# Fourth lead tile turned by a transposing transfer between B's two, lead filled with the third column tile and two input products of 384 tokens

## The chip, the cores and the metric

One core of a Trainium2 chip runs the whole kernel. The metric is the device time of one execution in microseconds (us). TensorE is called PE here, VectorE DVE, ScalarE ACT, GpSimd POOL; SP is the engine whose queue issues nearly all transfers.

## The reference

The input is x, 2048 tokens of 512 features in bf16. Three things are added up: x itself, a diagonal state-space layer (S5) on the normalised x, and a gated feed-forward network on the same normalised x.

```python
xn = (x - mean(x)) / sqrt(var(x) + 1e-5)              # per token, 2048 x 512
dt = exp(log_dt); Lam_bar = exp(dt * (Lambda_re + 1j * Lambda_im))
Bu = einsum("bld,pd->blp", xn, ((Lam_bar - 1) / Lam)[:, None] * (B_re + 1j * B_im))
h_t = Lam_bar * h_{t-1} + Bu_t                        # 2048 steps, 512 states
y = 2 * einsum("blp,dp->bld", h, C_re + 1j * C_im).real + xn * Dskip
ffn = (gelu(xn @ w_gate) * (xn @ w_up)) @ w_down      # inner width 1376
out = x + y + ffn
```

## The kernel before

The tokens are cut into 16 tiles of 128 and four blocks of four tiles. For every block the kernel makes the normalised tiles XN (tokens on partitions), turns them into XNT (features on partitions), and then runs three families of matmuls: GU (gate and up products, 11 column tiles of the inner width, line 787), Bu (the input products of the state-space layer, four row tiles of B's real part and four of its imaginary part, line 730) and DN (the down product with the state-space output added to it in the same bank, lines 860 and 871). ACT takes gate and up out of PSUM (Gelu and copy, lines 795 and 797), DVE multiplies them (line 799), rotates and scans the states (CHAIN, lines 758 to 779) and adds up the output (line 878).

The order of the work comes from a small planner in the kernel. Every operation is recorded with its engine, an assumed duration, and the buffers that it reads and writes; from the buffers the planner derives what waits for what. PE and SP keep the order in which the program records; DVE, ACT and POOL are put in order by due times, except where `S.pin` fixes the order by hand. Buffers can be declared in parts, so that a reader waits for the part alone: `XNTt[t]` is one turned tile, `XNTh[t][h]` half of one, `bank_part` a stretch of columns of a PSUM bank.

The first block is handled apart, since at the start everything has to be loaded. This is the lead:

- SP issues, in this order: the four x tiles of the first block (one transfer each), two parameter rows, gate and up chunk 1, `ld_tr(BBT[0], "A_B_re")` and `ld_tr(BBT[1], "A_B_im")` (transfers from memory that turn their 512x512 matrix on the way, line 483), gate and up chunk 2, the x tiles of the second block (`ld_x(4, 4)`), chunks 3 and 4, and the x tiles of the third block. Gate and up chunk 0 and a parameter row go by ACT's queue. A queue issues in order: an issue that waits holds up all that are behind it.
- `LN_lead` normalises the four tiles on DVE (lines 538, 539, 554, 567), with the square root on ACT or POOL.
- `TR_lead(tt)` turns a tile on PE: four transposes of 128x128 into PSUM (line 598), which ACT copies to XNT (line 607). All four lead tiles are turned so. Tiles 0 and 1 use two banks each, tile 2 bank 6, tile 3 bank 7.
- `lead_half` (line 620) makes GU products of column tiles 0 and 1 for one token tile, from one half of the features; `lead_mm(pairs, t0, t1, which)` makes GU products of the named column tiles for token tiles t0 to t1 (gate, up or both). Column tile k uses banks 2k and 2k + 1.
- `TR_par` turns the parameter rows into the second half of bank 7 (line 630); ACT reads them out there (lines 668 to 674).
- `BU(0)` then makes the eight input products, each of four matmuls of 512 columns (line 730), in the banks 6, 7, 0, 1, 2, 3, 4, 5: `bu_mm` the product, `bu_out` its eviction, the first two on ACT and six on DVE. The four products with B_re come first.

After the lead, `LN(1, False)` takes the statistics of the second block's tiles on DVE and normalises them, and `TR(1)` turns each of them by one transposing transfer from on-chip memory to on-chip memory on SP's queue (line 655); blocks 2 and 3 are turned in the same way.

Of the kernel before, what the change touches and what calls it, by code (L numbers as in the profile page):

```python
# [308 lines left out]
NT, NB, KD, KP, KF = 16, 4, 4, 4, 11  # L309
# [18 lines left out]
def d_act(n, ptr=0): return 100.0 + 0.833 * n + 90.0 * ptr  # L328


def build(nc, ins, out):
    with ExitStack() as es:
        E = es.enter_context
        S = Sched(nc, es)
# [26 lines left out]
        XNT = [Buf("XNT%d" % b, "xnt", 4 * b, 4 * b + 4, XNT_all.ap[:, b]) for b in range(NB)]  # L361
# [102 lines left out]
        def ld_x(t0, n, queue="sync"):  # L464
            return load(X_all.ap[:, t0:t0 + n, :], x2[128 * t0:128 * (t0 + n), :].rearrange("(j p) d -> p j d", p=128),
                        n * 128 * 1024, X[t0:t0 + n], "ld_x", queue)
# [15 lines left out]
        def ld_tr(dst, nm):  # L482
            return S.dma(lambda e: e.dma_start_transpose(dst.ap, ins[nm]), 4.0 * 1000 * 330, writes=[dst], tag="tr_" + nm,
                         issue=1900.0, lat=1000.0)

        def ld_gu(ci):
            ld_w(WG, WGc, ins["B_w_gate"], ci)
            ld_w(WU, WUc, ins["B_w_up"], ci)
# [7 lines left out]
        ld_param(2, "A_Lambda_im")  # L496
        ld_gu(1)
        ld_tr(BBT[0], "A_B_re")
        ld_tr(BBT[1], "A_B_im")
        ld_gu(2)  # L500
        ld_x(4, 4)
        ld_gu(3)
        ld_gu(4)
        ld_x(8, 4)

        def late_loads():
            load(WD.ap[:, 0:10, :], ins["B_w_down"][0:1280, :].rearrange("(k p) d -> p k d", p=128),
# [68 lines left out]
        def LN_lead():  # L576
            st = [stats(tt) for tt in range(4)]
            rs = {0: rsqrt_act(0)}
            ln = [[center_half(0), center_half(1)]]
            for tt in range(1, 4):  # L580
                if tt == 2:
                    rsqrt(RQt[0][tt], MVt[0][tt].ap[:, 1:2], [MVt[0][tt]], 1)
                else:
                    rs[tt] = rsqrt_act(tt)
                ln.append([center(tt)])
            S.pin(*st[0], *st[1], *ln[0], *ln[1], *st[2], *st[3], *ln[2], *ln[3])
            return rs

        def TR_lead(tt, after=()):
            banks = ((6, 7), (4, 5), (6,), (7,))[tt]  # L590
            nd, ne = KD // len(banks), (2, 2, 2, 4)[tt]
            parts = [bank_part(bank, 0, 256 * nd) for bank in banks]
            for h, bank in enumerate(banks):
                def f(e, h=h, bank=bank):
                    ins_ = None
                    for i in range(nd):
                        dk = nd * h + i
                        ins_ = e.transpose(PSH[bank][:, 128 * i:128 * i + 128], XN[tt].ap[:, 128 * dk:128 * dk + 128], IDN.ap)  # L598
                    return ins_
                S.op("tensor", f, 100 * nd, [XN0h[h] if tt == 0 else XN[tt], IDN], [parts[h]], "T0", after)  # L600
                if tt == 0:
                    warm_pe(1, (128, 384)[h], 3)
            ev = []
            for g in range(KD // ne):
                h, c0 = divmod(ne * g, nd)
                pt = PSH[banks[h]][:, 128 * c0:128 * (c0 + ne)]
                ev.append(ACT(lambda e, g=g, pt=pt: e.activation(  # L607
                    XNT[0].ap[:, ne * g:ne * g + ne, 128 * tt:128 * tt + 128], pt.rearrange("p (k t) -> p k t", k=ne), ACTF.Copy),
                    d_act(128 * ne), [parts[h]], [XNTt[tt] if ne == KD else XNTh[tt][g]], "evT"))
            return ev  # L610

        def lead_half(t, h, which=(0, 1)):
            c0, c1 = 128 * t, 128 * t + 128

            def f(e):
                ins_ = None
                for dk in range(2 * h, 2 * h + 2):
                    for k in range(2):
                        for i in which:
                            ins_ = e.matmul(PS[2 * k + i][:, c0:c1], (WG, WU)[i].ap[:, dk, 128 * k:128 * k + 128],  # L620
                                            XNT[0].ap[:, dk, c0:c1], start=(dk == 0), stop=(dk == KD - 1))
                return ins_
            PE(f, d_pe([128] * 4 * len(which)), [(WGc, WUc)[i][0] for i in which] + [XNTh[t][h]],
               [bank_part(2 * k + i, 4 * c0, 4 * c1) for k in range(2) for i in which], "GU0")
# [24 lines left out]
                    cs.append(center(tt))  # L649
            return cs  # L650

        def TR(b):
            for j in range(4):
                tt = 4 * b + j
                S.dma(lambda e, b=b, j=j, tt=tt: e.dma_start_transpose(
                    XNT[b].ap[:, :, 128 * j:128 * (j + 1)], XN[tt].ap),
                    300 * 1024, reads=[XN[tt]], writes=[XNTt[tt]], tag="tr_x", issue=1270.0, lat=1400.0)

        (TH, RRr, LBR, LBI, N1, TAa, TBb, DEN, RDEN, TC, TD, NRE, TE, TF, NIM, CR, CI) = range(17)
        pa = lambda i: PA[i].ap  # L660
# [65 lines left out]
        def bu_mm(b, s, c, bank, c0, c1, toks):  # L726
            def f(e):
                ins_ = None
                for dk in range(KD):
                    ins_ = e.matmul(PS[bank][:, c0:c1], BBT[c].ap[:, dk, 128 * s:128 * (s + 1)], XNT[b].ap[:, dk, c0:c1],  # L730
                                    start=(dk == 0), stop=(dk == KD - 1))
                return ins_
            PE(f, d_pe([c1 - c0] * KD), [BBT[c]] + toks, [bank_part(bank, 4 * c0, 4 * c1)], "Bu%d" % b)
# [4 lines left out]
                return V(lambda e: e.tensor_copy(ss.ap, PS[bank][:, :]), d_dve_1x(512), [BANK[bank]], [ss], "evBu", slack=1500.0)  # L738
            return ACT(lambda e: e.activation(ss.ap, PS[bank][:, :], ACTF.Copy), d_act(512), [BANK[bank]], [ss], "evBu", slack=1500.0)  # L739

        def BU(b, engs=("scalar",) * 8, banks=None):
            evs = []
            for i, (s, c) in enumerate((s, c) for c in range(2) for s in range(KP)):
                bank = banks[i] if banks else next_bank()
                bu_mm(b, s, c, bank, 0, 512, [XNT[b]])
                evs.append(bu_out(b, s, c, bank, engs[i]))
            return evs

# [44 lines left out]
        def gu_out(b, ft, bg, bu):  # L793
            m, k2, kk = FROWS[ft], b % 2, (KF * b + ft) % 3
            g = ACT(lambda e: e.activation(GG[kk].ap[0:m, :], PS[bg][0:m, :], ACTF.Gelu_apprx_tanh),  # L795
                    d_act(512), [BANK[bg]], [GG[kk]], "gelu", after=GATE["gelu"], slack=1500.0)
            u = ACT(lambda e: e.activation(UPB[kk].ap[0:m, :], PS[bu][0:m, :], ACTF.Copy),  # L797
                    d_act(512), [BANK[bu]], [UPB[kk]], "evU", slack=1500.0)
            h = V(lambda e: e.tensor_tensor(HTt[k2][ft].ap[0:m, :], GG[kk].ap[0:m, :], UPB[kk].ap[0:m, :], ALU.mult),  # L799
                  d_dve_tt2x(512), [GG[kk], UPB[kk]], [HTt[k2][ft]], "hmul")  # L800
            return g, u, h
# [83 lines left out]
        def warm_pe(n, cols=512, bank=0):  # L885
            def f(e):
                ins_ = None
                for _ in range(n):
                    ins_ = e.matmul(PS[bank][:, 0:cols], ONES[:, 0:128], ONES[:, 0:cols], start=True, stop=True)
                return ins_  # L890
            PE(f, 0.84 * cols * n, [], [BANK[bank]], "warm")

        def lead_mm(pairs, t0, t1, which=(0, 1)):
            for k in pairs:
                gu_mm(0, k, 2 * k, 2 * k + 1, t0, t1, which)

        def preload(tag, fn=lambda e: e.preload_act_table(ACTF.Gelu_apprx_tanh)):
            op = ACT(fn, 1300, [], [], tag)
            op.silent = True
            return op  # L900

        ldln = preload("ld_ln", lambda e: e.preload_act_table_set("natural_log_exp_and_others"))
        rs = LN_lead()
        warm_pe(9)
        warm_pe(1, 256)
        evT = [TR_lead(0)]
# [6 lines left out]
        lead_half(1, 1)  # L913
        TR_par()
        exps, cps, dec, t3 = decay()
        lead_mm((2,), 0, 2, (0,))
        evT.append(TR_lead(2))
        lead_mm((2,), 0, 2, (1,))
        evT.append(TR_lead(3, (exps[0], cps[1])))
        lead_half(2, 0)  # L920
        lead_half(2, 1)
        gelu0 = preload("ld_gelu")
        GATE["gelu"] = [gelu0]
        S.pin(prm0, g0, u0, ldln, *rs[0], *rs[1], *evT[0], *evT[1], *rs[3], exps[0], cps[1], *evT[2], *evT[3],
              *exps[1:], cps[0], gelu0)
        S.pin(*dec)
        for k in range(2):
            lead_mm((k,), 3, 4)
            S.pin(*gu_out(0, k, 2 * k, 2 * k + 1)[:2])
        lead_mm((2,), 2, 4)  # L930
        S.pin(*gu_out(0, 2, 4, 5)[:2])
        sint, cost, gelu1, dtab = tables()
        GATE["gelu"] = [gelu1]
        S.pin(*dtab)
        evb = BU(0, ("scalar",) * 2 + ("vector",) * 6, (6, 7, 0, 1, 2, 3, 4, 5))
        S.pin(*evb[:2], t3, sint, cost, gelu1)
        rstate["n"] = 6
        POOL(lambda e: e.tensor_copy(WG.ap[:, :, F:F + 32], WU.ap[:, :, F - 32:F]), 500, [WUc[-1]], [WGx], "wx")
# [84 lines left out]
```

## Time and profile before

| | us |
|---|---|
| median of 3 runs | 178.94 (178.84 to 179.36) |
| the profiled execution | 178.9 |
| its span in the profile | 177.1 |
| PE busy | 173.7, 888 matmuls |
| DVE busy | 161.4 |
| ACT busy | 103.4 |

The span is the time from the first to the last instruction in the profile; the profiled execution took 1.8 us more than its span. The clock that PE was granted was 1.00 of full speed throughout. The transfer engines were busy in nine tenths of most of the time from 4.4 to 22 us and moved 12.38 MB in all. "Idle before" in a row of the profile is how long the engine stood still ahead of the instruction, with what released it; an arrow names the releaser.

### The profile page before, as it was taken

To read this page: it belongs to the slowest core of one execution; us is meant where nothing else is said; L and a number is where in the kernel's file an instruction comes from. 1 tells how busy PE (TensorE), PEld (TensorE's weight loads), DVE (VectorE), ACT (ScalarE), POOL (GpSimd) and SP (SyncE) were. 2 spreads that over 40 slices of the span, in tenths; PEclk is the share of its full clock that TensorE was granted. 3 is DMA by queue.
4 is the path that set the end of the run, shared out by engine and by line. 5 is a ranking of instruction groups with operands and counts; after the bars stand their busy time and mean duration, and the time that the engine had idled before them with its cause. 6 is when DMAs were issued, how large, how long until landed. Compare 5 with 4: busy or idle time off the path is not lost.

```text
span 177.1 us, 2440 instructions
## 1 busy us (share of the span) xinstructions
PE 173.7 (98%) x888; PEld 81.9 (46%) x888; DVE 161.4 (91%) x249; ACT 103.4 (58%) x201; POOL 9.6 (5%) x24
## 2 busy tenths in 40 slices
PE   8999999999999999999999999999999999999994
PEld 3784444444444444444444444444444444444453
DVE  5898999998989999999999999989998999999631
ACT  3699998999999999396667500046867610000000
POOL 5100210000001400300000000000000000000000
PEclk9999999999999999999999999999999999999999
DMA  5999935996000041242000000110000000002021
GB/s 163 248 215 343 263 63 116 314 194 145 0 0 4 0 89 30 89 105 44 4 2 0 0 0 0 63 61 0 0 0 0 4 0 0 0 30 89 4 84 34
DMA packets 26345, 12.38 MB, mean 70 GB/s; under 512 B 17662, under 2 KB 26334, under 8 KB 26334
## 3 DMA queue, kind: packets, MB, share of 16 engines
q1 hardware_dynamic: 25270, 11.71, 27.0%
q10 hardware_dynamic: 1064, 0.53, 1.1%
q8 instruction: 7, 0.11, 0.3%
q14 instruction: 4, 0.03, 0.1%
HBM read 6.46 MB, written 2.10 MB: 48 GB/s over the span
## 4 chain that ended last, share of the span: by engine, by line
PE 96%; DMA 1%; DVE 1%; ACT 0%; issue 0%
PE PS L787 38%; PE PS L860 21%; PE PS L871 16%; PE PS L730 16%; PE PS L819 2%; PE PS L620 2%; DMA arena<-in_A_x_dram 1%; PE PS L835 1%; DVE arena L538 1%; PE PS L598 1%; ACT arena L607 0%; DVE arena L539 0%; DVE arena L878 0%; DVE arena L567 0%; PE PS L630 0%
## 5 line engine op out<-in xcount | busy, mean ns | idle before, releaser
L787 PE MATMUL PS<-arena 128*128 128x512 bf16 (+2 forms) x328 | 67.7, 366 | 0.0
L787 PEld LDWEIGHTS PS<-arena 128*128 128x128 bf16 x328 | 31.1, 98 | 35.4 <-ACT arena L826 0.8
L860 PE MATMUL PS<-arena 128*128 128x512 bf16 (+2 forms) x187 | 39.0, 367 | 0.0
L769 DVE TENSOR_TENSOR_SCAN arena<-arena 128x512 bf16<-128x512 f32 x32 | 38.5, 1251 | 0.0
L871 PE MATMUL PS<-arena 128*128 128x512 bf16 (+2 forms) x136 | 28.6, 367 | 0.0
L795 ACT ACTIVATE arena<-PS 128x512 bf16<-128x512 f32 x40 | 24.0, 599 | 7.5 <-PE PS L787 5.0
L730 PE MATMUL PS<-arena 128*128 128x512 bf16 x128 | 28.3, 379 | 0.0
L860 PEld LDWEIGHTS PS<-arena 128*128 128x128 bf16 x187 | 17.9, 98 | 20.4
L739 ACT ACTIVATE arena<-PS 128x512 bf16<-128x512 f32 x26 | 15.1, 600 | 19.8 <-PE PS L730 19.8
L797 ACT ACTIVATE arena<-PS 128x512 bf16<-128x512 f32 x40 | 24.0, 600 | 4.6 <-PE PS L787 4.4
L871 PEld LDWEIGHTS PS<-arena 128*128 128x128 bf16 x136 | 13.0, 98 | 14.7
L730 PEld LDWEIGHTS PS<-arena 128*128 128x128 bf16 x128 | 12.5, 98 | 14.9
L758 DVE TENSOR_TENSOR arena<-arena 128x4096 bf16<-128x4096 bf16 x8 | 18.3, 2284 | 0.1
L759 DVE TENSOR_TENSOR arena<-arena 128x4096 bf16<-128x4096 bf16 x8 | 18.3, 2283 | 0.0
L878 DVE TENSOR_TENSOR arena<-PS,arena 128x512 bf16<-128x512 f32 (+2 forms) x17 | 11.0, 655 | 7.4 <-PE PS L871 5.7
L799 DVE TENSOR_TENSOR arena<-arena 128x512 bf16<-128x512 bf16 x40 | 16.0, 418 | 1.8 <-ACT arena L797 1.2
L849 DVE TENSOR_TENSOR arena<-arena 128x512 f32<-128x512 bf16 x16 | 10.6, 689 | 0.4
L760 DVE TENSOR_TENSOR arena<-arena 128x2048 bf16<-128x2048 bf16 x8 | 9.8, 1221 | 0.2
L645 ACT ACTIVATE arena<-arena 128x512 bf16<-128x512 bf16 x8 | 6.0, 807 | 1.9 <-POOL arena L638 1.9
L538 DVE BATCH_NORM_STATS2 arena<-arena 128x6 f32<-128x512 bf16 x8 | 5.2, 676 | 1.7 <-DMA arena<-in_A_x_dram 1.7
L848 DVE TENSOR_TENSOR arena<-arena 128x512 bf16<-128x512 bf16 x16 | 6.3, 418 | 0.0
L722 DVE SCALAR_TENSOR_TENSOR arena<-arena 128x512 bf16<-128x512 bf16 x8 | 5.8, 750 | 0.4 <-ACT arena L720 0.3
(76 smaller groups left out, 107.2 us busy)
## 6 DMA issues: line engine op xcount, KB each, us to landing
out_dram<-arena SPq DMA_DIRECT2D x15, 128.0 KB, 1.7
arena<-in_A_x_dram SPq DMA_DIRECT2D x3, 512.0 KB, 6.6
arena<-in_B_w_down_dram SPq DMA_DIRECT2D x1, 1280.0 KB, 6.7
arena<-in_B_w_gate_dram SPq DMA_DIRECT2D x2, 384.0 KB, 6.4
arena<-in_B_w_up_dram SPq DMA_DIRECT2D x2, 384.0 KB, 6.7
arena<-in_A_x_dram SPq DMA_DIRECT2D x4, 128.0 KB, 2.9
arena<-in_B_w_gate_dram ACTq DMA_DIRECT2D x1, 256.0 KB, 3.3
arena<-in_B_w_up_dram ACTq DMA_DIRECT2D x1, 256.0 KB, 4.7
```

The costliest lines, as they stand in the source:

```text
L730: ins_ = e.matmul(PS[bank][:, c0:c1], BBT[c].ap[:, dk, 128 * s:128 * (s + 1)], XNT[b].ap[:, dk, c0:c1], start=(dk == 0), stop=(dk == KD - 1))
L739: return ACT(lambda e: e.activation(ss.ap, PS[bank][:, :], ACTF.Copy), d_act(512), [BANK[bank]], [ss], "evBu", slack=1500.0)
L758: V(lambda e: e.tensor_tensor(TB.ap, ssb.ap, sin4, ALU.mult), d_dve_tt2x(4096), [ssb, SINT], [TB], tag, after=GATE["rot"])
L759: V(lambda e: e.tensor_tensor(TA.ap, ssb.ap, cos4, ALU.mult), d_dve_tt2x(4096), [ssb, COST], [TA], tag, after=GATE["rot"])
L769: V(lambda e, g=g, rb=rb, init=init: e.tensor_tensor_scan(g.ap, rb, g.ap, init, ALU.mult, ALU.add), d_dve_scan(512), [g, PA[RRr]] + ([CARc ...
L787: ins_ = e.matmul(PS[bank][0:m, c0:c1], W.ap[:, dk, 128 * ft:128 * ft + m], XNT[b].ap[:, dk, c0:c1], start=(dk == 0), stop=(dk == KD - 1))
L795: g = ACT(lambda e: e.activation(GG[kk].ap[0:m, :], PS[bg][0:m, :], ACTF.Gelu_apprx_tanh), d_act(512), [BANK[bg]], [GG[kk]], "gelu", after ...
L797: u = ACT(lambda e: e.activation(UPB[kk].ap[0:m, :], PS[bu][0:m, :], ACTF.Copy), d_act(512), [BANK[bu]], [UPB[kk]], "evU", slack=1500.0)
L799: h = V(lambda e: e.tensor_tensor(HTt[k2][ft].ap[0:m, :], GG[kk].ap[0:m, :], UPB[kk].ap[0:m, :], ALU.mult), d_dve_tt2x(512), [GG[kk], UPB[ ...
L860: ins_ = e.matmul(o_, HTt[k2][ft].ap[:, tok], WD.ap[:, ft, c0:c1], start=(ft == 0), stop=False)
L871: ins_ = e.matmul(o_, SSc[k3][s][c].ap[:, tok], CT[c][s].ap[:, c0:c1], start=False, stop=(s == KP - 1 and c == 1))
L878: V(lambda e, o_=o_, ko=ko: e.tensor_tensor(OUTB[ko].ap[:, c0:c1], o_, XD[ko].ap[:, c0:c1], ALU.add), d_dve_1x(c1 - c0), [part, XD[ko]], [ ...
```

## The change

The order of SP's issues is changed: the second transfer of B (`A_B_im`) and all loads behind it are issued after a new transposing transfer, `TR(0, (3,))`, which turns the fourth lead tile (`XN[3]`) from on-chip memory into `XNT`. It stands between B's two transfers. The four PE transposes of that tile and ACT's eviction of them are gone, and with them the use of bank 7's first half for the tile.

PE's order in the lead changes with it. The third column tile (`lead_mm((2,), ...)`) is done in smaller parts: gate for token tile 0 before the third tile is turned, gate for tile 1 and up for tiles 0 and 1 behind it, both for tile 2 after the third tile's `lead_half`. Two of the input products with B_re (row tiles 0 and 1, banks 6 and 7) are then begun for 384 tokens, the first three tiles. Only after that come the matmuls that need the fourth tile: column tiles 0, 1 and 2 for its 128 tokens, the last 128 columns of the two begun products, and the other six products as before. In ACT's order the eviction is left out and the reads of the parameter rows follow directly on the third tile's evictions.

```diff
         ld_tr(BBT[0], "A_B_re")
-        ld_tr(BBT[1], "A_B_im")
-        ld_gu(2)
-        ld_x(4, 4)
-        ld_gu(3)
-        ld_gu(4)
-        ld_x(8, 4)
...
         def TR_lead(tt, after=()):
-            banks = ((6, 7), (4, 5), (6,), (7,))[tt]
-            nd, ne = KD // len(banks), (2, 2, 2, 4)[tt]
+            banks = ((6, 7), (4, 5), (6,))[tt]
+            nd, ne = KD // len(banks), 2
...
-                    d_act(128 * ne), [parts[h]], [XNTt[tt] if ne == KD else XNTh[tt][g]], "evT"))
+                    d_act(128 * ne), [parts[h]], [XNTh[tt][g]], "evT"))
...
-        def TR(b):
-            for j in range(4):
+        def TR(b, js=range(4)):
+            for j in js:
                 tt = 4 * b + j
-                S.dma(lambda e, b=b, j=j, tt=tt: e.dma_start_transpose(
+                d = S.dma(lambda e, b=b, j=j, tt=tt: e.dma_start_transpose(
                     XNT[b].ap[:, :, 128 * j:128 * (j + 1)], XN[tt].ap),
                     300 * 1024, reads=[XN[tt]], writes=[XNTt[tt]], tag="tr_x", issue=1270.0, lat=1400.0)
+            return d
...
-        def BU(b, engs=("scalar",) * 8, banks=None):
+        def BU(b, engs=("scalar",) * 8, banks=None, begun=0):
...
-                bu_mm(b, s, c, bank, 0, 512, [XNT[b]])
+                bu_mm(b, s, c, bank, 384 if i < begun else 0, 512, [XNT[b]])
...
         rs = LN_lead()
+        S.pin(TR(0, (3,)), ld_tr(BBT[1], "A_B_im"))
+        ld_gu(2)
+        ld_x(4, 4)
+        ld_gu(3)
+        ld_gu(4)
+        ld_x(8, 4)
...
-        lead_mm((2,), 0, 2, (0,))
+        lead_mm((2,), 0, 1, (0,))
         evT.append(TR_lead(2))
+        lead_mm((2,), 1, 2, (0,))
         lead_mm((2,), 0, 2, (1,))
-        evT.append(TR_lead(3, (exps[0], cps[1])))
         lead_half(2, 0)
         lead_half(2, 1)
+        lead_mm((2,), 2, 3)
+        for i in range(2):
+            bu_mm(0, i, 0, 6 + i, 0, 384, XNTt[0:3])
...
-        S.pin(prm0, g0, u0, ldln, *rs[0], *rs[1], *evT[0], *evT[1], *rs[3], exps[0], cps[1], *evT[2], *evT[3],
-              *exps[1:], cps[0], gelu0)
+        S.pin(prm0, g0, u0, ldln, *rs[0], *rs[1], *evT[0], *evT[1], *rs[3], exps[0], cps[1], *evT[2], *exps[1:], cps[0], gelu0)
         S.pin(*dec)
-        for k in range(2):
+        for k in range(3):
             lead_mm((k,), 3, 4)
             S.pin(*gu_out(0, k, 2 * k, 2 * k + 1)[:2])
-        lead_mm((2,), 2, 4)
-        S.pin(*gu_out(0, 2, 4, 5)[:2])
...
-        evb = BU(0, ("scalar",) * 2 + ("vector",) * 6, (6, 7, 0, 1, 2, 3, 4, 5))
+        evb = BU(0, ("scalar",) * 2 + ("vector",) * 6, (6, 7, 0, 1, 2, 3, 4, 5), 2)
```

## Prediction

> **What bounds the kernel now.** I read the page's busy line and its chain of work that ended last, then that chain in order of time, then the timelines of the sync queue (SP) and of the engines from 5 to 32 us, then the table of DMA issues and the DMA share in stretches of 0.2 us.
>
> ```profile
> PE 173.7 (98%) x888; PEld 81.9 (46%) x888; DVE 161.4 (91%) x249; ACT 103.4 (58%) x201; POOL 9.6 (5%) x24
> PE 96%; DMA 1%; DVE 1%; ACT 0%; issue 0%
> ```
>
> TensorE (PE) is the bound: 96% of the chain is PE. In the chain by time (start us, us, what) the stretch that the change touches is
>
> ```profile
> 8.02 0.44 PE PS L787 x4
> 8.46 0.22 PE PS L598 x4
> 8.68 0.44 PE PS L787 x4
> 9.12 0.22 PE PS L598 x4
> 9.34 0.89 PE PS L620 x16
> 10.24 1.77 PE PS L787 x24
> 12.00 6.91 PE PS L730 x32
> 18.91 12.09 PE PS L787 x56
> ...
> 170.66 1.79 PE PS L860 x11
> ```
>
> The pieces join without a gap, from here to the end of the kernel. So PE work taken away here is won whole, and a PE wait added here is lost whole: nothing later can absorb it. Prices per matmul: 128 columns 0.89/16 = 0.0555 us, a transpose (L598) 0.22/4 = 0.055, 256 columns 0.11, 384 columns 1.79/11 = 0.163, 512 columns 6.91/32 = 0.216.
>
> The suppliers, from the timeline (start, duration, queue or engine), the table of issues (last number: us from issue to landing), and the view of line 655:
>
> ```profile
> 4.97 2.54 SPq L483 DMA_TRANSPOSE arena<-in_A_B_re_dram  x1
> 7.56 1.75 SPq L483 DMA_TRANSPOSE arena<-in_A_B_im_dram  x1
> 7.57 0.86 DVE L554 TENSOR_SCALAR arena<-arena 128x512 bf16<-128x512 bf16 x2 [0.23 <-POOL arena L559]
> 11.15 0.51 SPq L462 DMA_DIRECT2D arena<-in_A_x_dram  x1
> 11.84 7.07 PE L730 MATMUL PS<-arena 128*128 128x512 bf16 x32
> ...
> 23.19 5.12 SPq L655 DMA_TRANSPOSE arena<-arena  x4
> arena<-in_A_B_re_dram SPq DMA_TRANSPOSE x1, 5.7
> arena<-in_A_B_im_dram SPq DMA_TRANSPOSE x1, 5.1
> DMA to landing us min/median/max: 2.4/2.5/3.1
> ```
>
> B_re lands at 4.97 + 5.7 = 10.67 and B_im at 7.56 + 5.1 = 12.66. The first B product starts at 11.84, the first one with B_im 4 x 0.864 = 3.46 later at 15.30, so PE waits for neither. The normalised fourth tile (XN3, second of the two L554) is ready at 7.57 + 0.86 = 8.43.
>
> **The change, part by part.** I count in matmul starts: the first L787 started at 7.86 by the timeline, the GU matmuls after the B products at 18.75, 10.89 us later.
>
> *PE work.* Before, those 10.89 us held 8 transposes 0.44, 16 half-tile matmuls L620 0.89, 8 of 256 columns 0.88, 24 more 1.77 and the B products 6.91. After: 64 of 128 columns (4 + 4 + 16 + 8 in the lead, 24 for the three column tiles' last 128 tokens, 8 for the rest of the two begun products) 3.55; 4 transposes 0.22; 4 of 256 columns 0.44; 8 of 384 columns 1.30; 24 of 512 columns 5.18: 10.70. The change saves **0.19 us**: the four transposes less the cost of cutting work smaller.
>
> *Wait for B_re.* The two begun products are now reached after 4 x 0.0555 + 0.22 + 4 x 0.0555 + 0.44 + 16 x 0.0555 + 8 x 0.0555 = 2.43 us, at 10.29; B_re lands at 10.67. With 0.05 to be seen, PE starts at 10.72 and loses **0.43 us**. The cover that hid this transfer (1.77 us of L787) now stands behind it. By the chain's clock, which runs 0.16 later than the starts (12.00 against 11.84), it would be 0.25; if B_re lands earlier with no second transfer queued behind it, nothing; if the new transfer steals from its tail, the 128 KB it moves, which line 655's transfers move in about 0.65 us of packets, up to 1.1. I take 0.43, the row as it stands.
>
> *The new transfer.* SP used to issue B_im at 7.56; now it waits until 8.43 for XN3, issues at about 8.50 (in the row of 23.19 it issued 0.08 after its tile) for 5.12/4 = 1.28 us, and only then B_im, at 9.78. Landing 2.4 to 3.1 after issue: 10.9 to 11.6. If its data must follow B_re's, whose packets thin out at about 10.1, it is 10.1 + 0.65 + the 0.6 us that lay between last packet (25.2) and landing (23.19 + 2.6) of line 655's first transfer = 11.4. PE wants the tile after the eight 384-column matmuls, at 10.72 + 1.30 = 12.02. Price **nothing**, covered by 0.4 us or more; without cover it costs what it is late. The nearest rows on the long side are B's own, four times the size: 5.1 us, 13.6, a wait of 1.6. I stay by line 655, the same shape from the same memory.
>
> The Trainium skill (VectorE: DVE Perf Modes, "The three transpose paths" and "Rules for kernel authors") speaks against the change: for a 128x128 bf16 block it gives 390 ns on TensorE and 1309 ns by DMA, and advises TensorE wherever PSUM as destination is acceptable. As an estimate from that page, four blocks one after the other would be 5.2 us, landing at 13.7 and a wait of 1.7 us; the sum would then be about 180.8. The trace disagrees twice: a transpose costs 55 ns in the stream, and a four-block transfer landed in 2.5 us.
>
> *B_im, moved by 2.2 us.* Issued at 9.78, by its own 5.1 it lands at 14.9, by B_re's 5.7 at 15.5. It is wanted after 24 + 8 matmuls of 128 columns (1.78) and 8 of 512 (1.73): 12.02 + 3.51 = 15.53. Nothing, but with the thinnest cover after B_re. The far row is the C transfer at 8.8 us, behind 1.3 MB of loads that do not stand here: 18.6, 3.1 us lost. Behind SP's wait stand B_im, then gate and up chunk 2, the second four x tiles, chunks 3 and 4 and the third four x tiles, all some 2.2 us later. Up chunk 2 (issued 10.60, 5.6 to landing) goes from 16.2 to 18.4; PE wants it at 18.99 + 0.86 = 19.85. Gate chunk 2 goes from 15.1 to 17.3, wanted at 18.99.
>
> *The x tiles 4 to 7.* They landed at 11.15 + 6.6 = 17.75, and VectorE's statistics began at 17.73, on their arrival; 5.46 us later SP issued the first of the four transfers of 23.19, and the last landed at 27.03 + 2.6 = 29.6, against the first product of the second block at 31.70. 2.2 us later: landing 19.95, and with the same 5.46 us the last tile turned at 31.8, against a demand that itself moves to 31.94. In the changed order two things shorten this path: the evictions of banks 0 to 4 now stand ahead of the statistics and the 0.64 us eviction between statistics and aggregation behind them. That makes it about 31.0. Nothing, with a cover of 1 us; the bank that VectorE empties after the statistics (bank 5, about 23.5) is wanted at 25.0.
>
> *ScalarE and the banks.* ScalarE loses one eviction of 512 columns (about 0.6 us). So its reads of the parameter rows in bank 7, which ended at 10.45 + 0.20 = 10.65, end near 10.1, and the second begun product, in that bank, is wanted at 11.4. The first Gelu eviction moves from 11.96 to about 12.5, when bank 0's last 128 tokens are done; it takes 0.6, and the third product wants bank 0 at 13.80. Nothing, with 0.6 us of cover, and later banks have more.
>
> *Sum:* -0.19 + 0.43 = **+0.24 us**. The profiled execution took 178.9 (span 177.1 and 1.8 around it), 0.04 below the median of 178.94, so after is 179.1 to 179.2; I say **179.15**.
>
> **The rivals.**
>
> 1. *No wait for B_re.* Its tail may have been slowed by B_im's issue, which is now later: after 8.85 its packets moved at 180 GB/s, against 290 before. Against it: its rate in that tail falls long before the second transfer's packets start at 10.4. Then -0.19: 178.75, chance 0.12.
> 2. *Slower: turning transfers do not overlap on the chip.* If the new one starts only when B_re has landed and takes its usual 2.5 us, it lands at 13.17 and PE waits 1.15 us more: 180.3. It decides from a landing later than 12.02. For: between B_re's last packets and B_im's first the DMA engines were nearly idle (share 0.04 at 10.20 to 10.40). Against: B_im landed only 2.0 us after B_re with four times the data, and line 655's four follow each other every 1.28 us while each takes 2.5. Chance 0.20. The four blocks one after the other of the Trainium skill (VectorE: DVE Perf Modes, "The three transpose paths") would be this case with 13.7 for 13.17; its chance lies in the 0.20.
> 3. *B_im late.* 0.7 us of cover by its own row, none by B_re's; an issue that stretches to B_re's 2.54 us, or a landing of 6.3, puts PE 0.5 to 0.8 us behind: about 179.8. Chance 0.13.
> 4. *The second block's tiles late.* The idle stretch between the new transfer and B_im shifts every load by 2.2 us; if the path through VectorE keeps its 5.46 us and B_im stretches too, PE stops before the second block's products for 0.3 to 0.7 us: 179.65. Chance 0.10.
>
> **How the numbers follow.** The forecast itself holds 0.45, with its own range 178.9 to 179.5. The range to 180.4 takes in rival 2, the low end 178.65 rival 1. A measurement here can tell about 0.3% (0.54 us) from no change: 178.40 to 179.48. The PE work saved is only 0.19, so faster than 178.40 needs something no row shows: 0.04. Same: 0.40 of the forecast's 0.45, 0.08 of rival 1, 0.05 of rival 4: 0.53. Slower: rivals 2 and 3, 0.05 of the forecast and 0.05 of rival 4: 0.43.
>
> **What would show it.** In the profile after: the 384-column matmuls start at 10.7, with PE idle some 0.4 us before them and B_re landing named as what ended it; the new transfer issued at 8.5 and landed by 11.6; B_im issued at 9.8, landed by 15.5; no idle PE at 12, 15.5, 19 or 31.9; the GU matmuls start at 19.0 instead of 18.75. PE idle at 12.0 ahead of the last 128 tokens is rival 2, at 15.5 rival 3, ahead of the second block's B products rival 4. I am wrong if the GU matmuls start before 18.75 or after 19.3.

## The result, and the profile after

| | before | after |
|---|---|---|
| median, us (22 executions each, same chip) | 179.03 (178.82 to 179.43) | 179.63 (178.76 to 180.27) |
| the profiled execution | 178.9 | 180.0 |
| its span | 177.1 | 178.2 |

The ratio is 1.003, 95% interval 1.0021 to 1.0039: the change costs 0.6 us, just above the 0.54 us that a measurement of this kernel can tell from no change, with that bound inside the interval. The times of after are in two groups with nothing between 179.22 and 179.55: seven executions at 178.76 to 179.22, where before's times lie, and fifteen at 179.55 to 180.27. The profile is one of the second group, so it shows what separates them.

The page of after, its busy line and its chain of work that ended last:

```profile
PE 173.2 (97%) x889; PEld 82.2 (46%) x904; DVE 161.6 (91%) x249; ACT 102.9 (58%) x200; POOL 10.8 (6%) x24
PE 88%; DMA 5%; ACT 4%; issue 1%; ACTq 1%; DVE 0%
```

PE's busy time fell by 0.5 us, but 15 matmul records are missing (889 against 904 weight loads), so this is not a gain. What counts is the chain: it was 96% PE and 1% DMA, and is 88% and 5% now (4.83 us of the DMA part are up chunk 0, early in the lead, and 4.30 us the new transfer). The same chain in order of time names the place (start us, us, what):

```profile
8.51 4.30 DMA arena<-arena
12.80 0.04 issue
12.85 0.41 PE PS L782 x4
```

Line 782 is 787 of before, 725 is 730, 649 is 655, 624 is 630, 614 is 620, 592 is 598 and 548 is 554. The chain leaves PE and runs for 4.30 us through the new transfer. The timeline of after (start, duration, queue or engine) shows what stands around it:

```profile
8.04 0.39 PE L782 MATMUL PS<-arena 128*128 128x128 bf16 x4
...
8.51 1.19 SPq L649 DMA_TRANSPOSE arena<-arena  x1
...
9.74 2.50 SPq L483 DMA_TRANSPOSE arena<-in_A_B_im_dram  x1
...
10.04 0.61 PE L782 MATMUL PS<-arena 128*128 128x128 bf16 x8
...
10.48 1.46 PE L725 MATMUL PS<-arena 128*128 128x384 bf16 x8
...
12.85 1.51 PE L782 MATMUL PS<-arena 128*128 128x128 bf16 x24 [0.90 <-DMA arena<-arena]
...
14.20 5.79 PE L725 MATMUL PS<-arena 128*128 128x128 bf16 x31
...
19.83 0.38 PE L782 MATMUL PS<-arena 128*128 128x512 bf16 x1
```

and the table of DMA issues of after (last number: us from issue to landing) gives the landings:

```profile
arena<-in_A_B_re_dram SPq DMA_TRANSPOSE x1, 4.8
arena<-in_A_B_im_dram SPq DMA_TRANSPOSE x1, 4.6
```

B_re landed at 4.96 + 4.8 = 9.76, before its first matmul at 10.48, which has no idle time in its row. The new transfer landed at 8.51 + 4.30 = 12.81. B_im landed at 9.74 + 4.6 = 14.34; the rows at 14.20 and 19.83 have no idle time either.

The two rows of before against which this is read are the first GU matmuls of this stretch and those behind the B products:

```profile
7.86 0.60 PE L787 MATMUL PS<-arena 128*128 128x256 bf16 x4
...
18.75 12.25 PE L787 MATMUL PS<-arena 128*128 128x512 bf16 x56
```

Where the time of this profile went: the GU matmuls behind the B products started at 18.75 before and 19.83 after, +1.08, nearly all of the span's +1.1. The first L782 starts at 8.04 against 7.86, +0.18; PE stood 0.24 us for up chunk 0 ahead of it, and that start varies from profile to profile for both kernels. The begun products were done at 10.48 + 8 x 0.163 = 11.78 and the next matmul started at 12.85: +1.07. (The row says 0.90, since it counts from the modelled end of the last matmul.) The saved PE work is -0.19. These make +1.06; 0.02 are left.

### The profile page after: what moved, and what is told of

The parts are those of the page before. It is cut to its first block, busy times and chain, and to the rows that moved or that the text cites. A ratio compares the mean times of both kernels' runs of the same rounds, so it can differ in the third digit from the quotient of the medians.

```text
span 178.2 us, 2456 instructions
## 1 busy us (share of the span) xinstructions
PE 173.2 (97%) x889; PEld 82.2 (46%) x904; DVE 161.6 (91%) x249; ACT 102.9 (58%) x200; POOL 10.8 (6%) x24
## 4 chain that ended last, share of the span: by engine, by line
PE 88%; DMA 5%; ACT 4%; issue 1%; ACTq 1%; DVE 0%
PE PS L782 36%; PE PS L855 21%; PE PS L866 15%; PE PS L725 12%; DMA arena<-in_B_w_up_dram 3%; DMA arena<-arena 2%; PE PS L814 1%; PE PS L830 1%; ACT arena L790 1%; ACT arena L734 1%; PE PS L614 1%; ACT arena L792 1%; ACT arena L541 0%; ACT arena L537 0%; ACTq L480 0%
## 5 line engine op out<-in xcount | busy, mean ns | idle before, releaser
L782 PE MATMUL PS<-arena 128*128 128x512 bf16 (+1 forms) x335 | 67.6, 359 | 1.2 <-DMA arena<-arena 0.9
L782 PEld LDWEIGHTS PS<-arena 128*128 128x128 bf16 x340 | 31.4, 98 | 36.6 <-DMA arena<-arena 1.3
L855 PE MATMUL PS<-arena 128*128 128x512 bf16 (+2 forms) x183 | 38.5, 366 | 0.2
L866 PE MATMUL PS<-arena 128*128 128x512 bf16 (+2 forms) x134 | 28.5, 366 | 0.1
L725 PE MATMUL PS<-arena 128*128 128x512 bf16 (+2 forms) x132 | 28.3, 366 | 0.2
L734 ACT ACTIVATE arena<-PS 128x512 bf16<-128x512 f32 x26 | 15.2, 600 | 19.3 <-PE PS L725 19.2
L873 DVE TENSOR_TENSOR arena<-PS,arena 128x512 bf16<-128x512 f32 (+2 forms) x17 | 10.8, 652 | 6.6 <-PE PS L866 5.4
L844 DVE TENSOR_TENSOR arena<-arena 128x512 f32<-128x512 bf16 x16 | 10.6, 688 | 0.4
```

The costliest lines, as they stand in the source:

```text
L782: ins_ = e.matmul(PS[bank][0:m, c0:c1], W.ap[:, dk, 128 * ft:128 * ft + m], XNT[b].ap[:, dk, c0:c1], start=(dk == 0), stop=(dk == KD - 1))
L855: ins_ = e.matmul(o_, HTt[k2][ft].ap[:, tok], WD.ap[:, ft, c0:c1], start=(ft == 0), stop=False)
L866: ins_ = e.matmul(o_, SSc[k3][s][c].ap[:, tok], CT[c][s].ap[:, c0:c1], start=False, stop=(s == KP - 1 and c == 1))
L873: V(lambda e, o_=o_, ko=ko: e.tensor_tensor(OUTB[ko].ap[:, c0:c1], o_, XD[ko].ap[:, c0:c1], ALU.add), d_dve_1x(c1 - c0), [part, XD[ko]], [ ...
```

## The experiments

All ratios are against the kernel before on the same chip, in five rounds each. Unless another is named, the edit is to the kernel after. The question is why a transfer that lands 2.4 to 3.1 us after its issue in blocks 1 to 3 of before took 4.3 here. The trace marks a transfer complete in 16 shares, as many as there are transfer engines. In the profile of after, 15 shares of this one were marked complete at 10.77 to 10.91 and the last at 12.80, and a packet of another queue, q8, lies between. The DMA queues of after from 10.3 to 10.4 us (packets, MB, share of 16 engines in this 0.1 us):

```profile
q8 instruction: 1, 0.02, 79.2%
q1 hardware_dynamic: 39, 0.01, 36.1%
```

One packet of 16,384 bytes, of the kind that fetches instructions, took 0.792 x 16 x 0.1 = 1.27 us. There are seven such fetches in a span. The theories:

- **A**: the fetch and the first packets of B_im behind it together hold the last share, until B_im's later packets push it out. B_im is needed for it.
- **B**: the prediction's second rival: turning transfers do not overlap, the new one waits for B_re.
- **C, later called F**: the fetch alone. It occupies one transfer engine, and the share of the new transfer on that engine lands late if the fetch begins before this share is through. Executions in which it begins later lose nothing, and this makes the two groups.
- **G**: the landing varies for itself, whatever the fetch does.

### e2_no_bim: no transfer of B_im

The transfer of B_im is left out, and its products use B_re in its place, so the output is not the reference's.

```diff
-        S.pin(TR(0, (3,)), ld_tr(BBT[1], "A_B_im"))
+        TR(0, (3,))
...
-                    ins_ = e.matmul(PS[bank][:, c0:c1], BBT[c].ap[:, dk, 128 * s:128 * (s + 1)], XNT[b].ap[:, dk, c0:c1],
+                    ins_ = e.matmul(PS[bank][:, c0:c1], BBT[0].ap[:, dk, 128 * s:128 * (s + 1)], XNT[b].ap[:, dk, c0:c1],
```

> B's imaginary part is not loaded; the four products that need it are made from B_re, so the output's state-space part is another. Behind the new transfer stand only ordinary loads. Theory A: nothing holds the new transfer's last share beyond the fetch itself, landing 10.9 to 12.0, wait 0 to 0.2, ratio 0.9985 to 1.000 (the saving of 0.19 us shows). Theory B: landing 12.8, ratio 1.003 or more. Theory C: landing about 12.3 where the fetch hits, ratio 1.001 to 1.003.

Measured: 179.45 (178.81 to 180.07), ratio 1.0025 (1.001 to 1.0039); the times spread from before's up to 180.07, here without a gap between groups. So, by the times, a loss is there without B_im, where A had wanted 0.9985 to 1.000: **A falls**. Where the slow executions lost it no profile of this run shows. The profile is of an execution without the loss: issued at 8.55, landed 2.4 us later at 10.96, no idle PE ahead of the tile's matmuls, the fetch at 10.8. Under B it should have landed at 12 or later: evidence against B.

### e3_fill_only: PE's new order without the new transfer

SP issues in the order of before and PE turns the fourth tile, between the third column tile and the begun products (the lines that give `TR_lead` its fourth bank and ACT its eviction again are left out here).

```diff
+        ld_tr(BBT[1], "A_B_im")
...
-        S.pin(TR(0, (3,)), ld_tr(BBT[1], "A_B_im"))
...
+        evT.append(TR_lead(3, (exps[0], cps[1])))
```

> The new PE order (third column tile in parts, two products begun for 384 tokens) with the fourth tile turned on PE as before and SP's order as before. The recorded working: PE work 0.03 more than before, and B_re, with B_im directly behind it, lands at about 10.67 while PE is there at 10.5: wait 0.2, ratio 1.0013. Theory A says the same, since B_im's first packets hold B_re's completion as in the kernel before. Rival: B_re lands near 9.8 as in the changed kernel's profile whatever is behind it, no wait, ratio 1.0002.

Measured: 179.09 (178.94 to 179.26), ratio 1.0 (0.9992 to 1.0009), one group. B_re landed 5.1 us after its issue, at 10.06, ahead of the begun products at 10.71. The prediction's wait for B_re is not there, though A and the prediction's working had both asked for 0.2 us, and the reordered lead costs nothing that can be measured by itself: the loss belongs to the new transfer.

### e4_gate_between: a load between the new transfer and B_im

```diff
-        S.pin(TR(0, (3,)), ld_tr(BBT[1], "A_B_im"))
-        ld_gu(2)
+        TR(0, (3,))
+        ld_w(WG, WGc, ins["B_w_gate"], 2)
+        ld_tr(BBT[1], "A_B_im")
+        ld_w(WU, WUc, ins["B_w_up"], 2)
```

> Gate chunk 2 (384 KB) is issued between the new transfer and B_im, up chunk 2 behind B_im. Theory A: B_im's first packets come after the gate's, at about 12.2, the new tile lands by 12.0, wait 0 to 0.3; B_im, issued at 10.3, lands at 15 to 15.9 against a demand at 15.4, wait 0 to 0.5; ratio 0.999 to 1.003, and PE's idle time stands at 15.4 rather than at 12. Theory B: wait 1.0 at 12, ratio 1.003 or more.

Measured: 180.0 (179.57 to 180.47), ratio 1.0043 (1.0029 to 1.0056). The transfer, issued at 9.02, landed 4.3 us later, with a fetch at 11.0, and PE stood 1.03 us for it. B_im was issued later than in after (10.88 against 9.74) and the landing was as late as there: a second miss for A, and no help from B_im's place in the queue. A variant with two loads of 1 KB in this place (e1_gap) has no measured time.

### e5_warm128 and e6_warm256: the fetch moved by more instructions

The warm-up ahead of the lead, 9 matmuls of 512 columns on constants, becomes 36 of 128 or 18 of 256: the same PE time in more instructions, so that a fetch tied to the count of PE's instructions comes earlier. The edit of e5, and that of e6 below it:

```diff
-        warm_pe(9)
+        warm_pe(36, 128)
...
-        warm_pe(9)
+        warm_pe(18, 256)
```

> The changed kernel with the nine warm-up matmuls of 512 columns cut into 36 of 128: the same columns, but 27 more matmuls and 27 more weight loads, so that TensorE reaches any given number of instructions about 1.5 us sooner. Theory F (a 16 KB instruction fetch, set off by TensorE's instruction count, keeps one transfer engine busy for 1.0 to 1.4 us from about 10.3 to 11.4, and where it begins before the new transfer's last packets, that engine's share lands 1.1 us after the fetch ends): the fetch starts at about 9, ends by 10.3, the tile lands by 11.5, PE does not wait before the last 128 tokens; ratio 0.9985 to 1.0005, spread as small as before's. Rival G (the new transfer's landing varies for itself, 2.4 to 4.3 us, in its place behind B_re): ratio 1.002 to 1.004 and the same spread of 1.5 us as the changed kernel.

> The changed kernel with the warm-up as 18 matmuls of 256 columns: 9 more matmuls and weight loads, the fetch about 0.5 us sooner. Theory F: the fetch starts at 9.8 to 10.9, nearly always ahead of the new transfer's last packets, so more executions are hit, each by less: landing about 12.0 to 12.5, wait 0.2 to 0.7, ratio 1.001 to 1.004, spread under 1 us. Rival G: ratio 1.002 to 1.004 with the spread of 1.5 us.

Measured: e5 179.32 (178.99 to 180.34), ratio 1.0027 (1.0013 to 1.0041); e6 179.65 (178.77 to 180.68), ratio 1.0038 (1.002 to 1.0055). In e5 the fetch moved to 9.1, as F said, but the time did not fall to before's, which F had also said: a miss. The timeline of e5 shows why. The fetch now fell into the start of the transfer, whose issue took 2.32 us instead of 1.19, and the tile was still late, by less. All that SP issues behind it came later too, and PE stood a second time, ahead of the second block's B products (32.23 against 31.70 in before):

```profile
8.47 2.32 SPq L649 DMA_TRANSPOSE arena<-arena  x1
...
11.94 1.51 PE L782 MATMUL PS<-arena 128*128 128x128 bf16 x24 [0.18 <-DMA arena<-arena]
...
32.23 7.07 PE L725 MATMUL PS<-arena 128*128 128x512 bf16 x31 [0.19 <-DMA arena<-arena]
```

In e6 the fetch stood at 10.4, the landing was 4.0 and PE stood 0.75 us. F had wanted the spread of e6 below 1 us; it is 1.9. In these two profiles, moving the fetch within the transfer did not free it.

### e7_before_warm128: the same warm-up in the kernel before

The edit is to the kernel before:

```diff
-        warm_pe(9)
+        warm_pe(36, 128)
```

> Control: the kernel before with the warm-up in 36 matmuls of 128 columns. Nothing in it waits closely for a transfer, so all theories say ratio 0.9995 to 1.0005; anything else is the price of the shorter warm-up matmuls and has to be taken off the run of the changed kernel.

Measured: 178.99, ratio 1.0 (0.9991 to 1.0008). The other warm-up costs nothing, so e5 and e6 may be read against before. But the fetch stood at 11.7, as in before (11.8), and not earlier: the count of instructions alone does not set the time of this first fetch. This was not cleared up; in both kernels B_im's packets pass at that time.

### e8_after_again: the kernel after, unchanged

> The changed kernel once more, on the chip of the three others and with a second profile. Theory F: where the new transfer lands late, one of its sixteen shares is late and the fetch began before 10.5; where the fetch begins after 10.9 it lands at 10.9 to 11.0 and PE does not wait. Ratio 1.002 to 1.004 in all theories.

Measured: 179.32 (178.84 to 179.63), ratio 1.0016 (1.0004 to 1.0027), a little under the 1.002 that all theories had said: six executions at 178.84 to 179.16 and six at 179.49 to 179.63. Its profile has the fetch at 10.1, a landing of 4.0 and 0.61 us of waiting. The loss comes and goes from one execution of the same kernel to the next.

### e9_swap: the tile that PE turns and the tile that the transfer turns change places

Tile 3 is loaded and normalised ahead of tile 2 in DVE's order, so that the transfer's tile is ready earlier; the gate product of the third column tile is one piece of 256 columns again.

```diff
-        for t in range(4):
+        for t in (0, 1, 3, 2):
...
-            S.pin(*st[0], *st[1], *ln[0], *ln[1], *st[2], *st[3], *ln[2], *ln[3])
+            S.pin(*st[0], *st[1], *ln[0], *ln[1], *st[3], *st[2], *ln[3], *ln[2])
```

> The changed kernel with tiles 2 and 3 of the lead changing places on VectorE: x tile 3 is loaded, measured and normalised before tile 2, so the new transfer can be issued some 0.45 us sooner (about 8.05), and the gate products of the third column tile for tiles 0 and 1 are one piece of 256 columns again, which stands ahead of tile 2's transposes and puts the instruction fetch some 0.2 us later. Theory F: the transfer's last packets pass at about 10.1, ahead of the fetch at 10.4 to 11; it lands at 10.4 to 10.6, PE does not wait at 12, and the 0.19 us of saved PE work shows: ratio 0.998 to 0.9995, spread as small as before's. Rival G (the transfer's landing varies for itself, up to 4.3 us after issue): it lands up to 12.4, ratio 1.000 to 1.003, spread over 1 us.

Measured: 179.35 (179.13 to 181.36), ratio 1.0032 (1.0011 to 1.0052). The transfer, issued at 8.12, landed 2.4 us later at 10.53, only 0.6 after B_re at 9.95. So the second turning transfer does not wait until the first has landed: **B falls**. The fetch came at 11.6, and nothing waited for the tile. The time was lost elsewhere, so that F's forecast of 0.998 to 0.9995 missed: on the tile that PE turns, which is now the late one. The timeline of e9:

```profile
8.46 0.41 DVE L548 TENSOR_SCALAR arena<-arena 128x512 bf16<-128x512 bf16 x1 [0.37 <-ACT arena L663]
...
8.93 0.40 PE L592 MATMUL PS<-arena 128*128 128x128 bf16 x4 [0.26 <-DVE arena L548]
```

### e10_late_fetch and e12_up_merge: the fetch moved by fewer instructions

In e12 the up products of the second column tile for token tiles 0 and 1 are one piece of 256 columns instead of two of 128: four matmuls fewer. e10 does this, and the same with the gate products of the third column tile: eight fewer. The first part of the diff is in both, the second in e10 alone.

```diff
-        lead_half(0, 0, (1,))
-        lead_half(0, 1, (1,))
-        lead_half(1, 0)
-        lead_half(1, 1)
+        lead_mm((0,), 0, 1, (1,))
+        lead_half(1, 0, (0,))
+        lead_half(1, 1, (0,))
+        lead_mm((0,), 1, 2, (1,))
+        lead_mm((1,), 0, 2, (1,))
...
-        lead_mm((2,), 0, 1, (0,))
+        lead_mm((2,), 0, 2, (0,))
         evT.append(TR_lead(2))
-        lead_mm((2,), 1, 2, (0,))
```

> The changed kernel, SP's order and the new transfer as they are, with eight fewer matmuls and weight loads ahead of the begun products: the up products of column tile 1 for token tiles 0 and 1, and the gate products of column tile 2 for the same two, are made in one piece of 256 columns instead of two of 128. TensorE's columns are the same; it reaches the fetch about 0.45 us later. Theory F: the fetch starts at 10.6 to 11.4, behind the new transfer's last packets at 10.5; the tile lands at about 10.9 in most executions, PE does not wait, and the 0.19 us of saved PE work shows, less up to 0.1 us because tile 2's transposes come 0.2 us later: ratio 0.9985 to 1.0005, and most executions in the lower group of the changed kernel's times. Rival G: ratio 1.002 to 1.004, spread 1.5 us.

> The changed kernel with four fewer matmuls and weight loads in the lead: the up products of column tile 1 for token tiles 0 and 1 in one piece of 256 columns. Tile 2's transposes stay where they are, and so does the order of the begun products, so the 0.2 us eviction wait of e10 and the B_re wait of e11 should both be absent. Theory F: the fetch starts at 10.6 to 11.3, behind the new transfer's last packets in most executions, no wait at 12; ratio 0.999 to 1.0005, spread under 0.8 us. If four are too few, part of the executions are still hit: ratio 1.001 to 1.002 and two groups of times. Rival G: ratio 1.002 to 1.004.

Measured: e10 179.22 (179.04 to 179.62) against 178.92, ratio 1.0018 (1.0009 to 1.0027). The fetch came at 11.8, the transfer landed 2.4 us after its issue, nothing waited for the tile, and the spread fell from after's 1.51 us to 0.58. The late group is all but gone, as F said (one execution of eleven is above 179.55), but the ratio is above F's 0.9985 to 1.0005; the 0.3 us that remain are put down, from the profile alone, to the third tile's half products (line 614, at 9.42 instead of 9.14) and to waits for gate and up chunks.

e12 took 179.04 (178.86 to 181.08) against 179.10, ratio 1.0009 (0.9985 to 1.0033): nine executions at 178.86 to 179.22, as the lower group of after, then 179.90 and 181.08. The two late ones have no profile, and the spread of 2.2 us is far from the 0.8 that F had wanted. The timeline of e12 is what this stretch should have looked like:

```profile
10.54 1.46 PE L725 MATMUL PS<-arena 128*128 128x384 bf16 x8
...
11.84 1.50 PE L782 MATMUL PS<-arena 128*128 128x128 bf16 x24
...
13.18 5.79 PE L725 MATMUL PS<-arena 128*128 128x128 bf16 x32
...
18.81 1.46 PE L782 MATMUL PS<-arena 128*128 128x512 bf16 x6
```

No row of this stretch has idle time. The difference to after is best seen side by side, in stretches of 0.2 us (window; its length; busy time of PE, PEld, DVE, ACT, POOL with instructions; granted PE clock; DMA share; GB/s). After:

```profile
10.20:10.40 0.20, 0.20 (x8) 0.20 (x5) 0.20 (x2) 0.20 (x1) 0.00 (x0) 1.00 0.99 210
10.40:10.60 0.20, 0.20 (x6) 0.18 (x4) 0.20 (x1) 0.20 (x1) 0.00 (x0) 1.00 0.06 4
```

and e12:

```profile
10.20:10.40 0.20, 0.20 (x8) 0.20 (x5) 0.20 (x2) 0.20 (x1) 0.00 (x0) 1.00 0.45 91
10.40:10.60 0.20, 0.20 (x7) 0.20 (x5) 0.20 (x2) 0.20 (x1) 0.00 (x0) 1.00 0.02 0
10.60:10.80 0.20, 0.20 (x4) 0.14 (x2) 0.20 (x2) 0.20 (x1) 0.00 (x0) 1.00 0.42 82
```

The lone burst of e12 after 10.6 is the fetch: 82 GB/s x 0.2 us = 16.4 KB, when the transfer's packets have ended. In after the same 1.27 us of one engine, 1.27 / (16 x 0.2) = 0.40, lie in the 0.99 of the first window, among the transfer's last packets.

What e12's profile gained here it did not keep. The last tile of the second block landed at 31.7, and PE, which wanted it 0.87 us after the start of line 814 (as in before, 30.83 to 31.70), stood some 0.18 us for it. Besides, line 624 had started 0.24 us later than in before (8.04 against 7.80). Together these are more than the saving:

```profile
30.90 1.03 PE L814 MATMUL PS<-arena 128*128 128x512 bf16 x4
31.95 7.07 PE L725 MATMUL PS<-arena 128*128 128x512 bf16 x32
```

### e11_begun_first: the begun products ahead of the third tile's GU products

```diff
-        lead_mm((2,), 2, 3)
         for i in range(2):
             bu_mm(0, i, 0, 6 + i, 0, 384, XNTt[0:3])
+        lead_mm((2,), 2, 3)
```

> The changed kernel with one exchange in TensorE's order: the two begun products of 384 tokens come before the third column tile's products for token tile 2, not behind them. The same instructions; but between 10.0 and 11.3 us TensorE now issues long matmuls, so that it reaches the instruction that sets off the fetch about 0.5 us later. B_re, which landed at 9.5 to 9.8 wherever the new transfer stood behind it, is wanted at 10.04. Theory F: the fetch starts at 10.8 or later, behind the new transfer's last packets; the tile lands at about 10.9, no wait at 12, and the 0.19 us of saved PE work shows: ratio 0.9985 to 1.0000, spread as small as before's (0.6 us). Rival G: ratio 1.002 to 1.004, spread 1.5 us.

Measured: 179.15 (178.72 to 179.85), ratio 1.0008 (0.9996 to 1.002), against F's 0.9985 to 1.0000. The transfer landed 2.4 us after its issue, the fetch came at 12.2, and nothing waited for the tile. In its place stands the wait that the prediction had put into the sum, since the begun products come 0.44 us earlier here and B_re landed at 10.3:

```profile
10.35 1.47 PE L725 MATMUL PS<-arena 128*128 128x384 bf16 x8 [0.35 <-DMA arena<-in_A_B_re_dram]
```

### What the profiles show together

The ten profiles of kernels with the new transfer, sorted by how long after its issue the fetch begins:

| kernel | issued | fetch begins, after the issue | landing after the issue | PE waits for the tile, by its row |
|---|---|---|---|---|
| e5 | 8.47 | 0.7 | 3.4 | 0.18 |
| e8 | 8.39 | 1.8 | 4.0 | 0.61 |
| after | 8.51 | 1.8 | 4.3 | 0.90 |
| e4 | 9.02 | 2.0 | 4.3 | 1.03 |
| e6 | 8.42 | 2.0 | 4.0 | 0.75 |
| e2 | 8.55 | 2.3 | 2.4 | 0 |
| e12 | 8.46 | 2.3 | 2.4 | 0 |
| e10 | 8.48 | 3.4 | 2.4 | 0 |
| e9 | 8.12 | 3.5 | 2.4 | 0 |
| e11 | 8.57 | 3.7 | 2.4 | 0 |

The split is clean: up to 2.0 us after the issue the landing is 3.4 to 4.3, from 2.3 us on it is 2.4 in all five. G would have mixed them.

The same profiles hold a second test without any transfer of B. The last of the twelve later turning transfers, issued at 80.2 to 81.5, has nothing of SP's behind it for more than 20 us. In five profiles a fetch begins 1.9 to 2.2 us after its issue, and it lands late: e2 4.0, e4, e8 and after 4.2, e11 4.3. In e9, e12 and e10 the fetch begins 2.4, 2.5 and 3.4 us after its issue, and it lands in 2.5. (PE does not wait for this tile.) The view of line 649 for this one transfer, in e11 and in e12:

```profile
L649 SPq DMA_TRANSPOSE arena<-arena x1: 1264/1264/1264, 80.2 to 80.2; - x1
DMA to landing us min/median/max: 4.3/4.3/4.3
...
L649 SPq DMA_TRANSPOSE arena<-arena x1: 1264/1264/1264, 80.2 to 80.2; - x1
DMA to landing us min/median/max: 2.5/2.5/2.5
```

So A, which needs B_im behind the transfer, and B, which needs B_re ahead of it, cannot be the cause there. F stands, for the landing. Its forecasts of times did much worse. The ratios of e5, e9, e10, e11 and e12 came out above what it had said (those of e11 and e12 by less than their intervals), and the spreads of e6 and e12 missed; in e5, e9, e11 and e12 the profiles show other waits in the place of this one. None of these kernels is faster than the one before.

## Why the prediction was right, and where it was wrong

The range and the bound were right; the way to the time was not. The result of 179.63 lies inside 178.65 to 180.4 but above the likeliest case's own 178.9 to 179.5. That is in part luck: the upper end stood there for rival 2, which did not occur. By the prediction's own sign it was wrong: it named GU matmuls after 19.3, and in the profile, which is of the upper group, they start at 19.83. Of the sum's terms one held, one was mis-sized, and a third, put at nothing, was the loss.

- **What bounds the kernel**: held. A PE wait at 12 us was lost whole; the GU matmuls, and the end, are as much later as the wait less the work saved.
- **PE work saved, 0.19 us**: held, and seen where nothing waits: in e12 the stretch from line 624 to the GU matmuls is 18.81 - 8.04 = 10.77 us, against 18.75 - 7.80 = 10.95 before. In the times of whole executions it shows in no variant.
- **Wait for B_re, 0.43 us**: mis-sized; the profile after shows 0. The step took one landing, 5.7 us, as fixed. In the other profiles it was 4.6 to 5.3 us (5.1 and 5.3 with B_im directly behind it too), and before's 5.7 was the longest of all. The step's mechanism is real: e11, which reaches the products earlier, waits 0.35 us by its row.
- **The new transfer, nothing**: this is the step that failed: "I stay by line 655, the same shape from the same memory". The shape is right: unhindered the transfer landed in 2.4 us in five profiles, as those rows say. But they were read as if a landing were a property of the shape. In the profile of before no fetch falls among the twelve transfers of those rows (they stand at 23 to 31, 62 to 68 and 75 to 82 us, its fetches at 11.8, 35.6, 57.4, 84.8 and later), so the rows could not show what a fetch does; what else uses the transfer engines at 10 us was asked of loads alone, not of q8, which the page lists with `7, 0.11, 0.3%`, a share too small to catch the eye. A fetch that begins 1.8 to 2.0 us after the issue makes it 4.0 to 4.3 us; the cover of 0.4 us and more is gone and PE loses 0.6 to 1.0 us.
- **Rival 2, not overlapping**: its price for the wait (1.15 us, 180.3) was near the 1.07 of the profile, its mechanism was not. PE idle at 12.0 was named as its mark, and that mark was there for another reason: e9's transfer landed 0.6 us after B_re. An idle row tells where and how much, not why. The Trainium skill (VectorE: DVE Perf Modes, "The three transpose paths") gives 1309 ns a block. The estimate worked out from it, 5.2 us for four blocks one after the other, is not borne out: the four blocks landed in 2.4 us where no fetch met them.
- **B_im 2.2 us later, nothing**: held. It was issued at 9.74 and landed at 14.34, in 4.6 us, about 1 us before PE would have wanted it even without the wait at 12 (11.78 + 3.51 = 15.29). Rival 3 did not occur.
- **The second block's tiles, ScalarE and the banks, nothing**: held. The second block's B products start at 32.78, directly behind the work ahead of them, with no idle row; rival 4 did not occur in after. But PE was a microsecond late there. In e12, where it was not, the last tile landed at 31.7 (issued at 28.5, 3.2 us to landing) and the cover of 1 us that the prediction reckoned was gone; in e5 the row names the wait. Part of that cover was a misreading: the last of the four transfers at 23.19 in before took 3.1 us to land, not 2.6, and so landed at 30.2, not at 29.6. Rival 4 is the next wait, of 0.2 to 0.4 us.
- **Rival 1, no wait for B_re**: its condition held in the profile of after; its time of 178.75 did not come. Even the lower group has a median of 179.12, 0.09 above before's.

So the forecast of +0.2 came from a wait that was not there, and the +0.6 from one in the upper group alone. What makes the two groups is only argued: after, e2, e4 and e8 give PE the same instructions, and there the fetch begins 2.3 to 2.6 us after line 624's matmul, which starts anywhere from 7.84 to 8.35, while the transfer's issue waits for its own tile. What stays open: what exactly starts the first fetch; that the queue serves PE is inferred from the counts below and from the shifts in e5, e10 and e12, and e7 did not shift; whether the late share is the one on the fetch's engine, since no view names a packet's engine; and why it lands about 1.1 us after the fetch has ended. A spacer between the transfer and the fetch, other than by instruction counts, has no measured run.

## What to carry to other kernels

A transfer whose landing has 0.4 us of cover needs the rows of everything that uses the transfer engines in its stretch, small queues too: a single 16 KB packet here was worth up to 1 us. Take a landing as a spread over all rows of its kind, not as one number; where times fall into two groups, profile each group and compare the shares of one transfer. And a mark that a rival predicts is no proof of it: move the suspected cause (here four matmuls) and see whether the mark goes. Then look at the next wait, too: taking this one away left the kernel no faster than before.

## What the runs showed of the hardware that was not expected

Instruction fetches share the transfer engines with data. Each of the seven per span moves 16,384 bytes as one packet that takes 0.9 to 1.6 us; a transfer that is complete in 16 shares has landed with its last one, so one fetch makes the landing 4.0 to 4.3 us instead of 2.4 or 2.5, on the last tile of the last block (e2, e4, e8, e11, after) as in the lead (e5, where it met the transfer's start: issue 2.32 us instead of 1.19, landing 3.4). Fetches come once per some 125 matmuls with their weight loads, that is per 250 instructions; 904 of both kinds in after, 1808 / 7 = 258. Counted by weight loads, two instructions each, the fourth fetch begins at instruction 902 to 910 of PE and the fifth at 1158 to 1164 in all thirteen profiles, whatever the kernel; the first, in the lead, comes anywhere from 182 to 268. The Trainium skill (Runtime: NRT & Kernel Launch, "Instruction fetch mechanics") has each engine's instruction store refilled in blocks of 16 KiB, 256 instructions, by a queue of its own; size and count here agree with it. It calls the cost of a block's boundary "mostly hidden". For the instructions themselves nothing here speaks against it, as no row names a fetch as what PE waited for; for the transfer that a fetch meets it does not hold.
